# The substitution of every chunk on GpSimd, two transposes of each as ScalarE copies, and the weights converted by their bits

## The chip, the core and the metric

One core of a Trainium2 chip runs the whole program. Its engines work side by side, each through its own queue in order: TensorE (PE; its weight loads are counted apart as PEld), VectorE (DVE), ScalarE (ACT) and GpSimd (POOL); SyncE (SP) issues the transfers. The metric is the time of one execution on the device in microseconds; lower is better.

## The reference

Two parts. The first is a linear attention with a decaying state of 40 x 40 for each of 4 x 8 heads, over 768 time steps:

```python
for t in range(S):
    y[:, :, t] = np.einsum('bhd,bhde->bhe', rt, state)
    Sa = np.einsum('bhde,bhe->bhd', state, at)
    state_decay = state * wt[:, :, None, :] - np.einsum('bhd,bhe->bhde', Sa, bt)
    state = state_decay + np.einsum('bhd,bhe->bhde', vt, kt)
```

The second takes y, laid out as x of (4, 768, 320), through a gated block: h = gelu(x @ w_in) of width 1024, split in halves u and v; v is normalized over its 512 columns and mixed over the 768 time steps by w_sg, with a bias; the result is x + (u * v) @ w_out. The weights w_in and w_out come as doubles (as pairs of 32-bit words) and are used as a high and a low part of 32 bits.

## The kernel before

**Chunks.** Time is cut into NCH = 12 chunks of C = 64 steps. In a chunk the 64 dependent steps become small matrix products and one triangular inverse for each of the 32 heads; two heads lie on the 128 partitions, so that 16 pairs lie side by side. The state goes from chunk to chunk.

**Gates.** For each chunk c and batch entry b (four a chunk) a gate is made, from `gate_w` to `gate_k`: a scan for the running products of the decays (`ex`), a reciprocal, products `at` and `kb` (each a VectorE or a GpSimd instruction, by a letter V or G in a table), then products on TensorE into `ab`, two masks back into `at` on VectorE (`gate_a`), the negated triangle `nts` on ScalarE (`gate_n`) and `kbt` (`gate_k`). `gate_3` ends with the load of the inputs of the gate four places later (`load_main`), which SyncE issues when that buffer is free.

**The inverse.** `inv_in` transposes `nts` into `n` on VectorE (all 16 pairs at once) and sets `x` to ones on the diagonal. Forward substitution of 32 steps then runs on `x`: `steps(c, lo, hi, eng, cuts, nm)` gives the steps lo to hi - 1 for one engine. On VectorE, the first steps (below ROWS[0] = 12) and the last (from 26) are single instructions that multiply and add (x<-n,x and x<-x,n in the profile); between them, and on GpSimd always, a step is a product into `tv` or `tg` and a sum. `both` puts the first FIRST = 3 steps of a chunk on VectorE, the next up to 29 on GpSimd, and the last LAST = 2 go to VectorE from `plan`. `inv_back` turns the result: k = 0 transposes `x` into `x1z`, k = 1 transposes that into the upper columns of `xt`, k = 2 and k = 3 transpose 32 partitions each into its lower columns. `inv_g` and `inv_x` make the remaining quarter of the 64 x 64 inverse by products (`gp`, `xp`).

**The chain of states.** `chain1` to `chain5` make, for each b, the corrected values (`ru`, `vu`), the new state (`sp`, `sc`) and the outputs (`pq`, `pqs`, `yp`, `yt`), which go to memory as `xd`.

**Order.** Each engine's order is written out by hand: every piece has a position in a table (CH, GPOS, START, BACK, GX), 28 units to a chunk, and `half` sorts them. The pieces before the first chunk's main part stand in one `merge`: `early` places the gates of chunks 0 and 1, `both` chunk 1's substitution, `zeros` and `blanks` the fills of buffers, at positions such as T0, T2, SECOND. Gates run about two chunks ahead of the chain, the inverse about one.

**The second part.** While the last three chunks run, `Mlp.side` loads and converts the twelve pieces of w_in (`DEC` gives each a position and the engine of its tail, `DSTEP` the positions of its stages), and starts on v. The rest (`run`) goes through a written sequence of products (`hv`, `hu`, `sg`, `op`), with eight pieces of w_out converted between (`OUTS`, `OSTEP`, `OUTE`). `split64` converts one piece: its words in `stg`, an exponent field cut out and clamped into `sc`, the upper fraction bits made a number by ScalarE and multiplied by the scale, the high part `h` taken by a rounding copy on ScalarE, and the rest added up as the low part `l`.

The profile calls nearly all instructions line 117, the helper `call` that keeps each engine in program order, so that tiles tell them apart.

Of the kernel before, what the change touches and what calls it, by code (L numbers as in the profile page):

```python
# [1072 lines left out]
```

## Time and profile before

| | |
|---|---|
| median of 3 runs | 689.81 us (689.4 to 694.77) |
| the profiled execution | 690.71 us |
| its span in the profile | 688.9 us |
| mean granted clock of TensorE | 0.906 |
| PE busy | 581.5 us (84%) |
| DVE busy | 561.5 us (82%) |
| ACT busy | 375.7 us (55%) |
| POOL busy | 363.0 us (53%) |

The shares are means over stages that differ: the start (0 to about 85 us), the steady chunks (to about 340), the last chunks beside the first pieces of the second part (to about 400), and the second part. Windows, timelines and waits are therefore read stage by stage. Times in the timelines are us from the span's start; a bracket behind a row gives the idle time of its engine before it, and what ended that.

### The profile page before, as it was taken

To read this page: it belongs to the slowest core of one execution; us is meant where nothing else is said; L and a number is where in the kernel's file an instruction comes from. 1 tells how busy PE (TensorE), PEld (TensorE's weight loads), DVE (VectorE), ACT (ScalarE), POOL (GpSimd) and SP (SyncE) were. 2 spreads that over 40 slices of the span, in tenths; PEclk is the share of its full clock that TensorE was granted. 3 is DMA by queue.
4 is the path that set the end of the run, shared out by engine and by line. 5 is a ranking of instruction groups with operands and counts; after the bars stand their busy time and mean duration, and the time that the engine had idled before them with its cause. 6 is when DMAs were issued, how large, how long until landed. Compare 5 with 4: busy or idle time off the path is not lost.

```text
span 688.9 us, 22501 instructions
## 1 busy us (share of the span) xinstructions
PE 581.5 (84%) x8950; PEld 523.2 (76%) x8950; DVE 561.5 (82%) x1294; ACT 375.7 (55%) x1082; POOL 363.0 (53%) x767
## 2 busy tenths in 40 slices
PE   6336798989989898898959788786699999999996
PEld 5235677877878777787848677685599999999995
DVE  7999889989889898898979776888868668766842
ACT  5445766968768687686654633652335324524410
POOL 5217687676866868567682552554632333233321
PEclk8556599999999999999978898978699999999998
DMA  6632233334433344332334332250003000200001
GB/s 219 208 96 64 66 93 109 108 89 112 126 102 108 89 120 115 99 90 70 97 99 117 100 88 69 81 152 9 19 18 99 1 30 20 78 30 2 29 24 40
DMA packets 57618, 56.55 MB, mean 82 GB/s; under 512 B 35936, under 2 KB 47456, under 8 KB 57504
## 3 DMA queue, kind: packets, MB, share of 16 engines
q1 hardware_dynamic: 57504, 55.02, 27.9%
q8 instruction: 72, 1.18, 0.7%
q14 instruction: 42, 0.34, 0.2%
HBM read 47.14 MB, written 7.86 MB: 80 GB/s over the span
## 4 chain that ended last, share of the span: by engine, by line
PE 41%; DVE 35%; ACT 11%; issue 5%; DMA 4%; POOL 2%; SPq 1%; POOLq 0%; DVEq 0%; ACTq 0%
PE sg L117 12%; PE op L117 6%; PE hu L117 5%; PE hv L117 5%; DVE at L117 4%; DVE x L117 4%; DVE sc L117 4%; PE ab L117 4%; PE yp L117 3%; DVE ex L117 3%; ACT nts L117 3%; DVE fixed L117 2%; DVE n L117 2%; PE sp L117 2%; DVE xt L117 2%
## 5 line engine op out<-in xcount | busy, mean ns | idle before, releaser
L117 POOL TENSOR_TENSOR tg<-x,n 128x126 f32<-128x126 f32 (+19 forms) x288 | 109.8, 381 | 76.8 <-DVE x L117 55.1
L117 POOL TENSOR_TENSOR x<-x,tg 128x126 f32<-128x126 f32 (+19 forms) x288 | 114.1, 396 | 22.6
L117 POOL TENSOR_TENSOR gx<-g,gy 128x384 fp32r<-128x384 f32 x32 | 33.4, 1047 | 79.5 <-ACT gy L117 79.5
L117 ACT ACTIVATE nts<-ab 32x256 f32<-32x256 f32 x192 | 62.0, 323 | 23.0 <-DVE at L117 20.7
L117 PE MATMUL ab<-at,kb 64*64 64x64 f32 x1536 | 42.5, 246 | 35.8 <-POOL kb L117 14.2
L117 PE MATMUL sg<-wsh,vh 128*128 128x384 f32 x192 | 67.0, 349 | 4.5 <-ACT vh L117 4.5
L117 PEld LDWEIGHTS ab<-at,kb 64*64 64x64 f32 x1536 | 34.6, 153 | 44.6 <-POOL kb L117 15.9
L117 PE MATMUL sg<-wsh,vl 128*128 128x384 f32 x192 | 67.0, 349 | 1.7 <-POOL vl L117 1.7
L117 PE MATMUL sg<-wsl,vh 128*128 128x384 f32 x192 | 66.9, 348 | 0.6 <-POOL wsl L117 0.6
L117 PE MATMUL pq<-rt,vut 128*128 128x128 f32 x384 | 58.8, 299 | 7.3 <-ACT kbt L117 4.1
L117 PEld LDWEIGHTS pq<-rt,vut 128*128 128x128 f32 x384 | 49.9, 202 | 12.6 <-ACT kbt L117 6.2
L117 PE MATMUL yp<-pqs,kbt 128*64 128x64 f32 x768 | 49.7, 234 | 6.7 <-DVE pqs L117 3.8
L117 ACT COPY vs<-sc 64x160 f32<-64x160 f32 x88 | 28.3, 321 | 46.2 <-DVE sc L117 45.1
L117 ACT CAST gy<-g 128x384 fp32r<-128x384 f32 x32 | 16.4, 513 | 66.8 <-DVE g L117 66.8
L117 PEld LDWEIGHTS yp<-pqs,kbt 128*64 128x64 f32 x768 | 42.1, 146 | 9.7 <-PE ut L117 3.8
L117 PE MATMUL yp<-rt,s 80*40 80x64 f32 x704 | 46.2, 231 | 0.0
L117 ACT CAST vh<-v 128x512 fp32r<-128x512 f32 x24 | 14.9, 621 | 56.2 <-DVE v L117 56.2
L117 DVE SCALAR_TENSOR_TENSOR g<-sg,gl,bt 128x384 f32<-128x384 f32 x32 | 19.7, 615 | 29.4 <-PE sg L117 28.4
L117 POOL TENSOR_TENSOR vl<-v,vh 128x512 fp32r<-128x512 f32 x24 | 31.3, 1304 | 21.9 <-ACT vh L117 21.9
L117 PEld LDWEIGHTS sg<-wsh,vh 128*128 128x128 f32 x192 | 37.9, 197 | 5.4 <-ACT vh L117 5.2
L117 POOL TENSOR_TENSOR rs<-rs,mhalf 128x1 f32<-128x1 f32 x24 | 13.4, 560 | 53.7 <-DVE rs L117 49.1
L117 PE MATMUL ru<-rhsb,xt 64*64 64x40 f32 x768 | 31.1, 239 | 12.4 <-ACT xt L117 11.2
(142 smaller groups left out, 1719.8 us busy)
## 6 DMA issues: line engine op xcount, KB each, us to landing
main<-main SPq DMA_DIRECT2D x88, 160.8 KB
vu<-vs SPq DMA_DIRECT2D x24, 160.0 KB
vs<-vb SPq DMA_DIRECT2D x24, 160.0 KB
rt<-rt SPq DMA_DIRECT2D x48, 80.0 KB
vut<-vt SPq DMA_DIRECT2D x24, 160.0 KB
xd<-yt SPq DMA_DIRECT2D x96, 40.0 KB
xt<-xd SPq DMA_DIRECT2D x16, 192.0 KB
out<-y SPq DMA_DIRECT2D x16, 192.0 KB
```

The costliest lines, as they stand in the source:

```text
L117: return self.tc.keep_in_program_order(f(*a, **k))
```

## The change

Three things, and the tables that place them.

1. **Substitution.** FIRST becomes 0 and T1, CUT0 and FIRST1 go: GpSimd does steps 0 to 28 of every chunk, chunk 0 and 1 too, VectorE the last two of each. In the part before the main loop VectorE makes chunk 1's gates with all their products, and the gates of b = 0 and 1 of chunk 2 (which leave the main loop's first rows of GPOS). The fills of `blanks` are placed from position 0 on.
2. **Transposes.** `inv_back` for k = 2 and 3 copies 32 partitions of `xt` from its upper to its lower columns on ScalarE, in place of the transposes from `x1z` on VectorE; k = 3 moves from position 18.09 to 24.7.
3. **Weights.** `split64` takes the magnitude of the upper word on ScalarE, clamps and shifts it, and puts sign and fraction together so that the word itself is a number; the multiplication of the upper part and the conversion of its fraction are gone. The stages are six in place of seven.

```diff
-FIRST = 3
-FIRST1 = 1
+FIRST = 0
-T1 = 16.9
-TB0 = 4.75
-TB1 = 12.31
-CUT0 = (0, 5, 16)
+TB0 = 0.0
+TB1 = 4.5
-BACK = (17.18, 23.28, 26.9, 18.09)
+BACK = (17.18, 23.28, 26.9, 24.7)
-DSTEP = ((-9.0, 0.0, 0.7, 1.4, 1.6, 2.4, 2.8), (-9.0, 0.0, 0.7, 1.4, 2.4, 4.0, 4.6))
+DSTEP = ((-9.0, -1.0, 0.0, 0.7, 1.4, 2.4), (-9.0, -1.0, 0.0, 0.7, 1.4, 3.0))
...
-                V.transpose(out=xt[r, :, 0:32], in_=x1_of[c][r])
+                A.copy(out=xt[r, :, 0:32], in_=xt[r, :, 32:64])
...
         merge(early(0, 0, EX[0], E0A, E0K, 1.0),
-              [(T0, lambda: inv_in(0))],
-              spread(steps(0, 0, 31, V, CUT0, "tv"), T0 + 0.05, T1),
-              early(1, T2, EX[1], E1A, E1K, EW),
-              both(1, FIRST1, *SECOND, "tw"),
+              both(0, 0, T0, 0.01),
+              early(1, T2, EX[1], "VVVV", "VVVV", EW),
+              both(1, 0, SECOND, 0.01),
+              early(2, THIRD, EX[1], "VV", "VV", EW),
               spread(zeros(), ZERO, ZERO + 1), spread(bl, TB0, TB1))
...
+        for f in steps(0, 31 - LAST, 31, V, (0, 16), "tv"):
+            f()
...
-                jobs = [(c + 3, 1)] if hf else [(c + 2, b) for b in ((0, 1, 2, 3) if c == 0 else (2, 3))] + [(c + 3, 0)]
+                jobs = [(c + 3, 1)] if hf else [(c + 2, b) for b in (2, 3)] + [(c + 3, 0)]
...
+        def size():
+            sc = z["sc"] = self.tmp("sc", n, I32)
+            A.activation(out=sc.bitcast(F32), in_=z["x"].bitcast(F32)[:, 1:2 * n:2], func=AF.Abs)
+
         def fields():
-            V.tensor_scalar(out=sc, in0=hi, scalar1=20, scalar2=0x7FF,
-                            op0=ALU.logical_shift_right, op1=ALU.bitwise_and)
-            V.tensor_scalar(out=sc, in0=sc, scalar1=896.0, scalar2=1151.0, op0=ALU.max, op1=ALU.min)
+            V.tensor_scalar(out=sc.bitcast(F32), in0=sc.bitcast(F32), scalar1=HI_MIN, scalar2=HI_MAX,
+                            op0=ALU.max, op1=ALU.min)
+            V.tensor_scalar(out=sc, in0=sc, scalar1=3, scalar2=0x3FFFFFF8,
+                            op0=ALU.logical_shift_left, op1=ALU.bitwise_and)
...
-            V.tensor_scalar(out=sc, in0=sc, scalar1=896.0, scalar2=float(2 ** 23), op0=ALU.subtract, op1=ALU.mult)
-            V.scalar_tensor_tensor(out=sc, in0=hi, scalar=-2 ** 31, in1=sc, op0=ALU.bitwise_and, op1=ALU.bitwise_or)
-            V.tensor_scalar(out=hi, in0=hi, scalar1=0xFFFFF, scalar2=None, op0=ALU.bitwise_and)
+            V.scalar_tensor_tensor(out=hi, in0=hi, scalar=-2 ** 30, in1=sc, op0=ALU.bitwise_and, op1=ALU.bitwise_or)
+            V.tensor_scalar(out=sc, in0=hi, scalar1=-2 ** 23, scalar2=None, op0=ALU.bitwise_and)
...
-            A.activation(out=z["m"], in_=z["x"][:, 1:2 * n:2], func=AF.Copy, scale=2.0 ** -20, bias=1.0)
             A.activation(out=z["r"], in_=z["lt"], func=AF.Copy, scale=2.0 ** -36)
-        def scaled():
-            s = z["sc"].bitcast(F32)
-            G.tensor_tensor(out=z["m"], in0=z["m"], in1=s, op=ALU.mult)
-            G.tensor_tensor(out=z["r"], in0=z["r"], in1=s, op=ALU.mult)
-        def high():
             A.copy(out=h, in_=z["m"])
         def low():
+            G.tensor_tensor(out=z["r"], in0=z["r"], in1=z["sc"].bitcast(F32), op=ALU.mult)
             G.tensor_tensor(out=z["m"], in0=z["m"], in1=h.bitcast(F32), op=ALU.subtract)
             G.tensor_tensor(out=l, in0=z["m"], in1=z["r"], op=ALU.add)
```

(In `split64`, G is the engine that the tables name for the piece: GpSimd or VectorE. OSTEP loses an entry in the same way as DSTEP, SECOND becomes one position, 14.0, and THIRD = 14.1 is new; GPOS and GE lose the two gates of chunk 2.)

VectorE's order behind the n of chunk 0, at the start of the program (nts_94 is chunk 0's triangle; ex_138, at_154 and main_85 belong to the first gate of chunk 1). Before:

```order
L117 STREAM_TRANSPOSE n<-nts_94 128x32x32
L117 SCALAR_TENSOR_TENSOR x<-n,x 128x31
L117 TENSOR_SCALAR call<-ex_138 128x4
L117 RECIPROCAL fixed_83<-call 128x4
L117 SCALAR_TENSOR_TENSOR x<-n,x 128x30
L117 SCALAR_TENSOR_TENSOR x<-n,x 128x29 x2
```

After:

```order
L115 STREAM_TRANSPOSE n<-nts_94 128x32x32
L115 TENSOR_SCALAR call<-ex_138 128x4
L115 RECIPROCAL fixed_83<-call 128x4
L115 TENSOR_TENSOR at_154<-main_85,ex_138 128x4x64
L115 SCALAR_TENSOR_TENSOR fixed_84<-main_85,fixed_83 128x260
L115 TENSOR_TENSOR kb<-main_85,fixed_84 128x2x4x64
```

The steps of the substitution have left this place, and the gate's two products, at and kb, have come to it from GpSimd.

GpSimd's order at its first step of a substitution; kbt_112 is the last buffer of the blank fills. Before, the chain that begins here is chunk 1's, from its second step on:

```order
L117 MEMSET kbt_112 128x24
L117 TENSOR_TENSOR tg_718<-x,n 128x30
L117 TENSOR_TENSOR x<-x,tg_718 128x30
L117 TENSOR_TENSOR tg_721<-x,n 128x58
L117 TENSOR_TENSOR x<-x,tg_721 128x2x29
```

After, it is chunk 0's, from its first:

```order
L115 MEMSET kbt_112 128x24
L115 TENSOR_TENSOR tg_407<-x,n 128x31
L115 TENSOR_TENSOR x<-x,tg_407 128x31
L115 TENSOR_TENSOR tg_410<-x,n 128x30
L115 TENSOR_TENSOR x<-x,tg_410 128x30
```

One chain more stands in GpSimd's queue, and each is longer by the steps that VectorE had.

ScalarE's order in a steady chunk, between the copies of the state (vs) of one pair of batch entries and the triangle (nts) of the next gate. Before:

```order
L117 COPY vs_114<-sc_122 64x4x40 x2
L117 COPY vut_130<-ut 80x4x64
L117 COPY gs_119<-gp 32x512 x2
L117 COPY vs_114<-sc_123 64x4x40 x2
L117 COPY vut_130<-ut 80x4x64
L117 ACTIVATE nts_96<-ab_2549 32x256
```

After:

```order
L115 COPY vs_114<-sc_122 64x4x40 x2
L115 COPY vut_130<-ut 80x4x64
L115 COPY gs_119<-gp 32x512 x2
L115 COPY xt_90<-xt_90 32x16x32
L115 COPY vs_114<-sc_123 64x4x40 x2
L115 COPY vut_130<-ut 80x4x64
L115 COPY xt_90<-xt_90 32x16x32
L115 ACTIVATE nts_96<-ab_2511 32x256
```

The two copies in place of the transposes stand in this stretch of ScalarE's queue, one behind gs and one ahead of nts.

More of the change, by code (lines that the diff above doesn't have):

```diff
@@ L30 @@
 DECAY_LOW = 1e-09
-FIRST = 3
-FIRST1 = 1
+HI_MIN = float(np.uint32(896 << 20).view(np.float32))
+HI_MAX = float(np.uint32(1151 << 20).view(np.float32))
+FIRST = 0
 EW = 1.41
@@ L35 @@
 T0 = 6.16
-T1 = 16.9
 T2 = 5.9
-TB0 = 4.75
-TB1 = 12.31
-CUT0 = (0, 5, 16)
+TB0 = 0.0
+TB1 = 4.5
 CH = ((0.37, 2, 4, 5.28, 4.96, 7.81, 8.16, 12.17, 3.28, 10.76, 13.17, 14.9), (-0.13, 1.6, 7.06, 5.51, 8.13, 6.96,
     10.2, 10.99, 2.92, 8, 12, 13.85))
-GPOS = (((0.34, 0.33, 0.61, 1.31, 3.87, 4.25, 4.26, 4.27), (2.6, 2.59, 2.87, 3.57, 5.89, 6.51, 6.52, 6.53), (5.06,
+GPOS = (((5.06,
     5.05, 5.33, 6.03, 8.35, 10.4, 10.41, 10.42), (8.18, 8.17, 8.83, 9.53, 11.85, 12.47, 12.48, 12.49), (10.81, 10.8,
@@ L47 @@
     2.69, 9.57, 13.23, 13.24, 13.25),), ((1.07, 1.06, 1.26, 1.42, 9.29, 11.98, 11.99, 12.0),))
-GE = ("VVVVV", "VVV", "V", "V")
+GE = ("VVV", "VVV", "V", "V")
 START = (13.13, 0.58)
@@ L51 @@
 E0K = "GVGG"
-E1A = "GGGG"
-E1K = "GVGG"
-BACK = (17.18, 23.28, 26.9, 18.09)
+BACK = (17.18, 23.28, 26.9, 24.7)
 GX = (24.68, 4.6)
@@ L75 @@
 OUTS = (10, 11, 12, 13, 14, 15, 16, 17)
-OSTEP = (-2, 0, 0, 0, 0, 1, 1)
+OSTEP = (-2, 0, 0, 0, 0, 1)
 SGE = "GVGVGVGVVVGG"
 OUTE = "GGGVGGGG"
-SECOND = (18.63, 0.02)
+SECOND = 14.0
+THIRD = 14.1
 ZERO = 4.0
@@ L520, in early @@
             out = []
-            for b in range(B):
+            for b in range(len(EA)):
                 for f, x in zip(PIECES, X):
@@ L684, in load @@
             self.Q.dma_start(out=z["x"], in_=src)
+        def size():
+            sc = z["sc"] = self.tmp("sc", n, I32)
+            A.activation(out=sc.bitcast(F32), in_=z["x"].bitcast(F32)[:, 1:2 * n:2], func=AF.Abs)
         def fields():
-            x = z["x"]
-            hi = x[:, 1:2 * n:2]
-            sc = z["sc"] = self.tmp("sc", n, I32)
-            V.tensor_scalar(out=sc, in0=hi, scalar1=20, scalar2=0x7FF,
-                            op0=ALU.logical_shift_right, op1=ALU.bitwise_and)
-            V.tensor_scalar(out=sc, in0=sc, scalar1=896.0, scalar2=1151.0, op0=ALU.max, op1=ALU.min)
+            sc = z["sc"]
+            V.tensor_scalar(out=sc.bitcast(F32), in0=sc.bitcast(F32), scalar1=HI_MIN, scalar2=HI_MAX,
+                            op0=ALU.max, op1=ALU.min)
+            V.tensor_scalar(out=sc, in0=sc, scalar1=3, scalar2=0x3FFFFFF8,
+                            op0=ALU.logical_shift_left, op1=ALU.bitwise_and)
         def scale():
@@ L699, in scale @@
                             op0=ALU.logical_shift_right, op1=ALU.bitwise_and)
-            V.tensor_scalar(out=sc, in0=sc, scalar1=896.0, scalar2=float(2 ** 23), op0=ALU.subtract, op1=ALU.mult)
-            V.scalar_tensor_tensor(out=sc, in0=hi, scalar=-2 ** 31, in1=sc, op0=ALU.bitwise_and, op1=ALU.bitwise_or)
-            V.tensor_scalar(out=hi, in0=hi, scalar1=0xFFFFF, scalar2=None, op0=ALU.bitwise_and)
+            V.scalar_tensor_tensor(out=hi, in0=hi, scalar=-2 ** 30, in1=sc, op0=ALU.bitwise_and, op1=ALU.bitwise_or)
+            V.tensor_scalar(out=sc, in0=hi, scalar1=-2 ** 23, scalar2=None, op0=ALU.bitwise_and)
         def parts():
             z["m"], z["r"] = z["x"].bitcast(F32)[:, 1:2 * n:2], z["lt"].bitcast(F32)
-            A.activation(out=z["m"], in_=z["x"][:, 1:2 * n:2], func=AF.Copy, scale=2.0 ** -20, bias=1.0)
             A.activation(out=z["r"], in_=z["lt"], func=AF.Copy, scale=2.0 ** -36)
-        def scaled():
-            s = z["sc"].bitcast(F32)
-            G.tensor_tensor(out=z["m"], in0=z["m"], in1=s, op=ALU.mult)
-            G.tensor_tensor(out=z["r"], in0=z["r"], in1=s, op=ALU.mult)
-        def high():
             A.copy(out=h, in_=z["m"])
         def low():
+            G.tensor_tensor(out=z["r"], in0=z["r"], in1=z["sc"].bitcast(F32), op=ALU.mult)
             G.tensor_tensor(out=z["m"], in0=z["m"], in1=h.bitcast(F32), op=ALU.subtract)
             G.tensor_tensor(out=l, in0=z["m"], in1=z["r"], op=ALU.add)
-        return load, fields, scale, parts, scaled, high, low
+        return load, size, fields, scale, parts, low
     def weights_in(self):
```

## The prediction, made before the result was known

> **What bounds the kernel now.** I read the windows of each stage first (columns: stretch, length, then busy time of PE, PEld, DVE, ACT, POOL, granted clock, DMA share, GB/s).
>
> ```profile
> 55.30:86.60 31.30, 25.68 (x460) 22.17 (x460) 28.33 (x63) 21.64 (x69) 22.32 (x60) 0.61 0.25 76
> 201.80:230.30 28.50, 25.70 (x656) 22.36 (x653) 26.45 (x61) 21.48 (x69) 20.18 (x53) 1.00 0.39 106
> 340.40:376.00 35.60, 27.55 (x602) 24.75 (x598) 29.96 (x77) 16.16 (x46) 22.47 (x51) 0.81 0.39 107
> 460.00:496.00 36.00, 24.43 (x106) 20.44 (x105) 31.68 (x69) 14.09 (x40) 21.08 (x33) 0.83 0.06 15
> 496.00:540.00 44.00, 44.00 (x231) 42.51 (x230) 34.19 (x68) 19.36 (x40) 13.55 (x15) 0.94 0.16 50
> ```
>
> VectorE (DVE) is the fullest engine up to 496 us; from there TensorE is busy in all 44.00 of 44 us, and its work is not changed. So what is won before 496 us moves the end one for one, and nothing after it does. One period of the scan (a chunk) is 28.5 us.
>
> Next the timeline of VectorE at the start (start, length, instruction, idle before it):
>
> ```profile
> 19.74 2.13 DVE L117 STREAM_TRANSPOSE n<-nts 128x1024 f32<-128x1024 f32 x1 [0.29 <-ACT nts L117]
> 49.09 2.53 DVE L117 SCALAR_TENSOR_TENSOR x<-x,n 128x14 f32<-128x14 f32 x15
> 54.23 1.04 DVE L117 STREAM_TRANSPOSE x1z<-x 128x512 f32<-128x512 f32 x1
> 57.34 0.69 DVE L117 TENSOR_TENSOR_SCAN ex<-main,fixed 128x260 f32<-128x260 f32 x1
> 60.02 0.69 DVE L117 TENSOR_TENSOR_SCAN ex<-main,fixed 128x260 f32<-128x260 f32 x1
> 62.91 0.74 DVE L117 TENSOR_TENSOR at<-ab,mask 64x256 f32<-64x256 f32 x2
> 85.51 1.07 DVE L117 STREAM_TRANSPOSE x1z<-x 128x512 f32<-128x512 f32 x1
> ```
>
> From the end of n (21.9) to the fifteen last small steps (49.09 + 2.53 = 51.6 us) VectorE does chunk 0's whole substitution and, between its steps, the gates of chunk 1. The row x1z marks the end of a chunk's substitution: chunk 0 at 54.23, chunk 1 at 85.51. GpSimd (POOL) meanwhile:
>
> ```profile
> 54.39 0.23 POOL L117 TENSOR_TENSOR tg<-x,n 128x30 f32<-128x30 f32 x1 [14.15 <-DVE x L117]
> 55.02 0.28 POOL L117 TENSOR_TENSOR tg<-x,n 128x58 f32<-128x58 f32 x1
> 79.62 0.28 POOL L117 TENSOR_TENSOR x<-x,tg 128x45 f32<-128x45 f32 x1
> 84.33 0.28 POOL L117 TENSOR_TENSOR tg<-x,n 128x56 f32<-128x56 f32 x1 [4.43 <-DVE x L117]
> 138.98 0.28 POOL L117 TENSOR_TENSOR tg<-x,n 128x56 f32<-128x56 f32 x1 [4.34 <-DVE x L117]
> ```
>
> It stands idle for 14.15 us before 54.39, and some 4.3 us in each period, waiting for VectorE's first steps.
>
> **The start.** Chunk 1's 28 steps took GpSimd 54.39 to 79.90 = 25.5 us (0.455 us an instruction, gaps included). One more step like the first, 0.63 us (54.39 to 55.02), makes a full chain of 29 steps 26.1 us. After the change it starts for chunk 0 when n is there, at 22.0 (the blank fills that are moved earlier stand in its idle time before that), and ends at 48.1. VectorE now makes chunk 1's four gates and two of chunk 2's meanwhile. A gate costs 57.34 to 60.02 = 2.7, and 0.7 for its two masks: 3.4 us. Six gates and one n (2.1) from 21.9 make 44.4; for the waits on ACT before n and on TensorE before the last masks I add 3.6, an estimate: 48. The two engines arrive together, and x1z of chunk 0 comes at 49.3 in place of 54.23. SyncE's queue now has the loads of two more gates (which wait for those gates' kb) ahead of chunk 0's vs, rt and vut; these leave at 46 to 52 us, as the first products ask for them, and I price that at 0 to 2 us.
>
> GpSimd goes on with chunk 1: 48.1 + 26.1 = 74.2, three last VectorE steps (0.9), x1z at 75.1 in place of 85.51. VectorE is there sooner: of the 31.3 us between its two x1z, two gates (6.8), two transposes (1.35) and four small steps (0.75; their rows follow) are gone, 49.3 + 22.4 = 71.7. So GpSimd ends last, and the start is worth **-10.4 us** (bounds -12, if the waits that follow chunk 1 shrink too, and -4, if TensorE, at a clock of 0.61 here and 25.68 of 31.30 us busy, paces it).
>
> **The steady periods.** What leaves VectorE in each:
>
> ```profile
> 201.85 0.70 DVE L117 STREAM_TRANSPOSE xt<-x1z 32x512 f32<-32x512 f32 x1
> 206.40 0.42 DVE L117 TENSOR_TENSOR yt<-yp,ex 128x256 f32<-128x256 f32 x1 [1.32 <-PE yp L117]
> 206.74 0.69 DVE L117 STREAM_TRANSPOSE xt<-x1z 32x512 f32<-32x512 f32 x1
> 223.13 0.23 DVE L117 SCALAR_TENSOR_TENSOR x<-n,x 128x31 f32<-128x31 f32 x1
> 223.62 0.68 DVE L117 SCALAR_TENSOR_TENSOR x<-n,x 128x30 f32<-128x30 f32 x3
> ```
>
> Transposes 1.35, steps 0.75 (their ends overlap what follows): 2.1 us of 28.5, with one idle gap of 1.32. What comes to ACT has no row; the nearest are its copies of as many elements:
>
> ```profile
> L117 ACT COPY xt<-xp 32x512 f32<-32x512 f32 x24 | 13.8, 573 | 2.3 <-PE xp L117 2.0
> L117 ACT COPY x<-x 128x512 f32<-128x512 f32 x12 | 7.4, 621 | 0.2
> ```
>
> 0.57 to 0.62 each; I take 0.58 with the first, 1.15 us a chunk. How much of the 2.1 shows is read from who waits:
>
> ```profile
> 196.17 1.32 ACT L117 ACTIVATE nts<-ab 32x256 f32<-32x256 f32 x4 [1.42 <-DVE at L117]
> 209.97 0.40 ACT L117 COPY at<-at 64x256 f32<-64x256 f32 x1 [0.30 <-DVE at L117]
> 211.42 0.78 PE L117 MATMUL ab<-at,kb 64*64 64x64 f32 x32 [0.69 <-ACT rhsb L117]
> 224.66 0.38 ACT L117 ACTIVATE nts<-ab 32x256 f32<-32x256 f32 x1 [1.23 <-DVE at L117]
> 203.54 0.67 PE L117 MATMUL sp<-vu,kbt 128*64 128x40 f32 x16
> 204.39 0.32 DVE L117 TENSOR_TENSOR sp<-sp,sc 104x160 f32<-104x160 f32 x1
> ```
>
> The four steps stand just ahead of the masks for which ACT waits 1.42: their 0.75 moves ACT, and TensorE behind it, forward in full. The first transpose lies beside a stretch where TensorE runs through to its sp, which ends at 204.2, 0.2 us before VectorE takes it up: only that much of the 0.70 is won. Then the two ACT copies come between the copies after gp and the nts that follow; ACT runs there without a gap up to 209.97, where its slack is 0.30. So TensorE's ab at 211.42, which waits for ACT, does not come forward by 0.9 but stays within 0.1, and VectorE, early by 1.5, waits there for about 1.0. At the end of the period all are ahead by 0.25 + 0.75 = **1.0 us**. From x1z of chunk 1 to that of chunk 10 there are nine periods: **-9.0 us** (bounds 0 and 9 x 2.1 = -19). GpSimd's chain of 26.1 fits the 27.5 that are left.
>
> ```profile
> 339.32 1.09 DVE L117 STREAM_TRANSPOSE x1z<-x 128x512 f32<-128x512 f32 x1
> ```
>
> **Conversion, and the last chunks.** Each of 20 pieces loses one VectorE instruction, and one multiplication on the engine that does its tail:
>
> ```profile
> L117 DVE TENSOR_SCALAR sc<-sc 128x256 int32<-128x256 int32 x32 | 13.7, 429 | 0.6
> L117 DVE TENSOR_TENSOR stg<-stg,sc 128x256 f32<-128x256 f32 x6 | 2.8, 468 | 3.6 <-ACT stg L117 3.6
> L117 POOL TENSOR_TENSOR stg<-stg,sc 128x256 f32<-128x256 f32 x10 | 8.6, 863 | 29.1 <-ACT stg L117 21.6 <-DMA xd<-yt 7.4
> ```
>
> That is at most 16 x 0.43 + 6 x 0.47 = 9.7 us of VectorE. ACT keeps its three instructions a piece (the magnitude replaces a conversion of the same size: nothing), but the high half is ready without the trip to the multiplying engine and back. Where it counts:
>
> ```profile
> 346.75 0.43 DVE L117 TENSOR_TENSOR stg<-stg,sc 128x256 f32<-128x256 f32 x1 [1.60 <-ACT stg L117]
> 349.93 0.43 DVE L117 TENSOR_TENSOR stg<-stg,wih 128x256 f32<-128x256 f32 x1 [1.57 <-ACT wih L117]
> 356.90 0.43 PE L117 MATMUL ru<-rhsb,xt 64*64 64x40 f32 x2 [6.75 <-ACT xt L117]
> 388.22 0.39 PE L117 MATMUL ru<-rhsb,xt 64*64 64x40 f32 x2 [4.06 <-ACT xt L117]
> ```
>
> TensorE stands 6.75 us because ACT's xt is queued behind the conversion of the second weight, which waits for VectorE. VectorE gets there earlier by two transposes (1.4), two small instructions (0.7), one multiplication (0.4) and one of the two ACT waits (1.6): 4.1, of which I count all, and 2 of the 4.06: **-6 us** (bounds 0 and -10.8, both stalls). Chunk 11's chain then ends near where VectorE asks for it, so more is not likely. Between 460 and 496 us VectorE is busy 31.68 of 36, with most of the w_out pieces there; their removed instructions are 3 to 4 us, of which I take **-3** (bounds 0 and -5).
>
> **Sum.** The profiled execution took 690.71 us (span 688.9). 690.7 - 10.4 - 9.0 - 6 - 3 = 662.3. That execution lies 0.9 above the median of the runs, 689.81, so I say **662**.
>
> **Rivals.** *GpSimd in VectorE's way.* Some VectorE instructions are longer beside a GpSimd one:
>
> ```profile
> 209.33 0.61 DVE L117 TENSOR_TENSOR at<-main,ex 128x256 f32<-128x256 f32 x1
> 225.89 0.41 DVE L117 TENSOR_TENSOR at<-main,ex 128x256 f32<-128x256 f32 x1
> ```
>
> The at at 225.89 came soon after a pause of GpSimd, the one at 209.33 in the middle of its chain; the pause shrinks from 4.3 to about 1 us. If five VectorE instructions a chunk lose 0.2 each, the period gains 1.0 - 1.0 = 0: 690.7 - 10.4 - 0 - 9 = 671, and with a start slowed alike 675. Against it: GpSimd is running beside most of them already. The Trainium skill, "SBUF — State Buffer", section "Who interferes with whom", says that a VectorE instruction with two SBUF inputs and a GpSimd one that reads SBUF exclude each other for a whole instruction; the two rows agree with it, and by it the time would be this rival's 671.
>
> *VectorE alone sets the time.* If the ACT copies hide, the whole 2.1 shows: 690.7 - 12 - 19 - 6 - 5 = 649. For it: 26.45 of 28.5 busy; against it: ACT's slack of 0.30.
>
> *GpSimd becomes the bound: slower.* If half of the 58 instructions of a chain met a VectorE one and lost 0.2, a chain took 31.9, the period 3.4 more, ten times: +34, the start +1, less 9 later: 717. From 12 such meetings a chunk (2.4 / 0.2) on GpSimd paces the period; from about 25 on the whole gain is lost. Against it: the chain of 54.39 to 79.90 ran beside a VectorE busy 28.33 of 31.30 us, and its 0.455 us is in my sum. The Trainium skill, "GPSIMD Engine Reference", section 3.1, has GpSimd about twice as slow as VectorE at such work; the chain's own rows set my price, and the rule only says that the work is not cheaper there.
>
> *The start does not gain* (TensorE at half clock or the loads pace it): 690.7 - 4 - 9 - 9 = 669.
>
> **How the numbers follow.** Chances: forecast 0.48 (655 to 668), GpSimd in VectorE's way 0.20 (668 to 677), start 0.10 (667 to 673), VectorE alone 0.15 (643 to 655), GpSimd the bound 0.05 (about 717), some mixture that cancels 0.02. A measurement of this kernel tells about 1% from no change. Faster by over 1% (below 683) is 0.92, within 1% 0.04, slower 0.04. The range that leaves out no more than 2 in 10 is 648 to 676.
>
> **What would show it.** Right: a first tg at 22 us and no pause before the second chain; x1z of chunk 0 near 49, of chunk 1 near 75, of chunk 10 near 320; a period near 27.5 with a new wait of VectorE for ab about ten us after x1z, and ACT without a gap before it; the stall before ru at the last chunk down to some 2 us; full TensorE from about 468 us. Wrong: a period of 28.5 or more, at of 0.61 throughout, an instruction of tg well above 0.46, or a start in which x1z of chunk 1 waits for anything but GpSimd.

## The result

The changed kernel takes 671.66 us in the median of its first four runs (668.41 to 674.49), the kernel before 691.14 in the runs beside them: a ratio of 0.971, 95% interval 0.964 to 0.978. Four later runs of it on another occasion gave 669.64 us, 0.971 again (0.965 to 0.977). The forecast was 662 in a range of 648 to 676.

The profile below is that of the run of 674.49 us (span 672.7), the longest of the eight; a second profile, of a run of 666.78 (span 665.0), stands beside it where the two differ. First the windows by stage (the columns are those of the prediction).

```profile
20.00:50.00 30.00, 13.87 (x216) 10.93 (x216) 25.00 (x53) 17.07 (x57) 22.68 (x61) 0.50 0.51 155
50.00:83.00 33.00, 27.37 (x454) 23.99 (x455) 21.86 (x44) 18.73 (x58) 27.08 (x75) 0.50 0.27 80
83.00:111.00 28.00, 26.62 (x560) 23.35 (x562) 21.82 (x50) 22.45 (x70) 19.28 (x53) 0.84 0.31 86
111.00:330.00 219.00, 202.93 (x5187) 177.87 (x5189) 192.52 (x425) 179.07 (x559) 172.78 (x464) 1.00 0.39 105
330.00:400.00 70.00, 62.12 (x1046) 56.04 (x1040) 44.04 (x115) 38.57 (x107) 34.98 (x68) 0.71 0.39 108
```

The same view of the second profile, three of its stages:

```profile
50.00:83.00 33.00, 27.53 (x455) 24.16 (x456) 21.70 (x44) 18.58 (x57) 27.09 (x75) 0.50 0.28 81
83.00:111.00 28.00, 25.67 (x619) 21.99 (x619) 24.15 (x54) 22.72 (x71) 20.99 (x58) 0.99 0.38 103
330.00:400.00 70.00, 59.54 (x1013) 53.24 (x1010) 47.87 (x121) 41.05 (x112) 34.44 (x67) 0.78 0.37 101
```

VectorE is no longer the fullest engine: from 50 to 83 us it is busy 21.86 of 33, and TensorE at half clock 27.37. The steady part does the same in both profiles; they differ where the granted clock does, from 83 to 111 and from 330 to 400 us.

Where the time went is read from marks that every profile has: the start of x1z of some chunks (VectorE's timeline), the first hv (TensorE's) and the span's end, in us.

| kernel | x1z chunk 0 | 1 | 2 | 10 | 11 | first hv | end |
|---|---|---|---|---|---|---|---|
| before | 54.23 | 85.51 | 115.23 | 339.32 | 372.56 | 408.61 | 688.9 |
| after, first profile | 49.82 | 79.68 | 111.41 | 327.77 | 358.23 | 394.32 | 672.7 |
| after, second profile | 49.66 | 79.52 | 109.11 | 325.34 | 355.98 | 388.38 | 665.0 |

From these come the terms of the prediction's sum. It took 10.4 up to chunk 1, and nine periods from there; here the first of these nine stands with the start.

| term | forecast | first profile | second profile |
|---|---|---|---|
| start, to x1z of chunk 2 | -11.4 | -3.8 | -6.1 |
| eight periods, chunk 2 to 10 | -8.0 | -7.7 | -7.9 |
| last chunks, chunk 10 to hv | -6 | -2.7 | -6.3 |
| w_out part, hv to the end | -3 | -1.9 | -3.7 |
| sum, from the marks unrounded | -28.4 | -16.2 | -23.9 |

The start is short in both. The other three are close to the forecast in the second profile. The forecast's -28.4 set beside the -19.5 of the first medians (691.14 to 671.66) and the -22.0 of the later ones (691.65 to 669.64) leaves 6 to 9 us to explain.

In the start GpSimd does what was said. Its chains, from its timeline:

```profile
22.55 0.50 POOL L115 TENSOR_TENSOR tg<-x,n 128x31 f32<-128x31 f32 x1 [5.79 <-DVE call L115]
49.05 0.24 POOL L115 TENSOR_TENSOR tg<-x,n 128x31 f32<-128x31 f32 x1
75.22 0.24 POOL L115 TENSOR_TENSOR tg<-x,n 128x31 f32<-128x31 f32 x1 [0.18 <-DVE n L115]
```

Chunk 0's chain starts at 22.55, chunk 1's follows at 49.05 without a pause, chunk 2's at 75.22: 26.2 us for chunk 1's, 26.1 forecast. But VectorE takes the end of chunk 1's up only at 78.91:

```profile
49.82 1.05 DVE L115 STREAM_TRANSPOSE x1z<-x 128x512 f32<-128x512 f32 x1
53.86 0.69 DVE L115 TENSOR_TENSOR kb<-main,fixed 128x512 f32<-128x512 f32 x1
62.42 0.33 DVE L115 TENSOR_TENSOR sp<-sp,sc 104x160 f32<-104x160 f32 x1 [7.87 <-PE sp L115]
78.91 0.73 DVE L115 SCALAR_TENSOR_TENSOR x<-x,n 128x15 f32<-128x15 f32 x3
79.68 1.07 DVE L115 STREAM_TRANSPOSE x1z<-x 128x512 f32<-128x512 f32 x1
84.86 0.33 DVE L115 TENSOR_TENSOR sp<-sp,sc 104x160 f32<-104x160 f32 x1 [1.89 <-PE sp L115]
88.23 0.33 DVE L115 TENSOR_TENSOR sp<-sp,sc 104x160 f32<-104x160 f32 x1 [2.67 <-PE sp L115]
111.41 1.09 DVE L115 STREAM_TRANSPOSE x1z<-x 128x512 f32<-128x512 f32 x1
```

It stands 7.87 us for sp of chunk 0, the end of a serial chain x1z, gp, xp, ru, sp that goes back and forth between TensorE and ACT. TensorE's timeline shows the chain:

```profile
51.08 1.93 PE L115 MATMUL ru<-vs,at 64*64 64x40 f32 x32 [2.41 <-DMA vs<-vb]
52.94 1.92 PE L115 MATMUL gp<-x1z,nts 64*32 64x32 f32 x64
55.53 0.31 PE L115 MATMUL xp<-xt,gs 64*32 64x32 f32 x2 [0.67 <-ACT gs L115]
58.76 0.43 PE L115 MATMUL ru<-rhsb,xt 64*64 64x40 f32 x2 [0.72 <-ACT xt L115]
61.22 1.08 PE L115 MATMUL sp<-vu,kbt 128*64 128x40 f32 x16
```

Two things in it could be shorter: gp stands behind the ru that waited for the load of vs until 51.08 (x1z was there at 50.87), and each product runs at a clock of 0.50.

### The profile page after: what moved, and what is told of

Same layout as the page of the kernel before. It is cut to its first block, busy times and chain, and to the rows that moved or that the text cites. A ratio compares the mean times of both kernels' runs of the same rounds, so it can differ in the third digit from the quotient of the medians.

```text
span 672.7 us, 22391 instructions
## 1 busy us (share of the span) xinstructions
PE 593.0 (88%) x8950; PEld 535.2 (80%) x8950; DVE 510.7 (76%) x1100; ACT 391.5 (58%) x1106; POOL 383.3 (57%) x866
## 5 line engine op out<-in xcount | busy, mean ns | idle before, releaser
L115 POOL TENSOR_TENSOR tg<-x,n 128x126 f32<-128x126 f32 (+21 forms) x348 | 127.8, 367 | 47.7 <-DVE n L115 10.6
L115 POOL TENSOR_TENSOR x<-x,tg 128x126 f32<-128x126 f32 (+21 forms) x348 | 133.6, 384 | 27.3
L115 PE MATMUL ab<-at,kb 64*64 64x64 f32 x1536 | 45.2, 250 | 30.3 <-DVE kb L115 17.0
L115 PEld LDWEIGHTS ab<-at,kb 64*64 64x64 f32 x1536 | 36.1, 156 | 40.7 <-ACT junk L115 14.0
L115 PE MATMUL pq<-rt,vut 128*128 128x128 f32 x384 | 61.6, 310 | 0.8 <-DVE yt L115 0.6
L115 PEld LDWEIGHTS pq<-rt,vut 128*128 128x128 f32 x384 | 53.2, 214 | 4.0 <-DVE yt L115 1.2
L115 ACT COPY vs<-sc 64x160 f32<-64x160 f32 x88 | 28.3, 321 | 38.6 <-DVE sc L115 37.7
L115 POOL TENSOR_TENSOR vl<-v,vh 128x512 fp32r<-128x512 f32 x24 | 31.3, 1303 | 21.5 <-ACT vh L115 21.3
L115 DVE TENSOR_TENSOR at<-ab,mask 64x256 f32<-64x256 f32 x96 | 35.9, 407 | 7.8 <-PE ab L115 7.3
```

Of the source, the lines that this page charges most:

```text
L115: return self.tc.keep_in_program_order(f(*a, **k))
```

## The experiments

Ratios are to the kernel before, run beside each on the same chip, with 95% intervals. "The changed kernel" has 0.971.

### The start

**The two gates of chunk 2 back behind chunk 0's x1z.**

```diff
-              early(2, THIRD, EX[1], "VV", "VV", EW),
...
-                jobs = [(c + 3, 1)] if hf else [(c + 2, b) for b in (2, 3)] + [(c + 3, 0)]
+                jobs = [(c + 3, 1)] if hf else [(c + 2, b) for b in ((0, 1, 2, 3) if c == 0 else (2, 3))] + [(c + 3, 0)]
```

(with their rows of GPOS and GE)

> The two early gates of chunk 2 go back behind x1z of chunk 0, everything else as after the change. Theory (behind x1z of chunk 0 the serial chain x1z, gp, gs, xp, xt, ru, vu, sp of 12.6 us sets the time, and VectorE stands 7.9 us in it): the two gates fill that idle time, x1z of chunk 0 comes at 46 to 50 us, x1z of chunk 1 within 1.5 us of the 79.7 measured, x1z of chunk 2 within 2 us of 111.4, and the whole within 2 us of the changed kernel. Rival (the gates moved ahead are a true gain of the start, and what is late is late for another cause): x1z of chunk 1 near 86 and the whole 6 to 7 us slower than the changed kernel, about 0.980 of the kernel before.

667.83 us, 0.967 (0.962 to 0.972), which can't be told from 0.971. x1z of chunk 1 comes at 79.68, to the hundredth as in the first profile of the changed kernel, that of chunk 2 at 109.25, near the second's 109.11. VectorE now makes the gates where it stood, and its wait for sp is 0.60 us in place of 7.87. So the 6.8 us of gates that the prediction took off VectorE there brought nothing: behind chunk 0's x1z not VectorE's work but the chain to sp sets the time, and the gates had only covered it. One thing more moves with them: without the two gates' loads ahead of it the load of vs is issued at 34.53 us in place of 46.85 (SyncE's timeline), and the first ru is out of gp's way. What that is worth is seen two runs below.

**Eight fillers a gate.** `warmup(8)`, eight products of a tile of zeros, behind each gate of chunks 0 and 1.

```diff
+            if c < 3 and FILL[c]:
+                warmup(FILL[c])
```

> Eight filler matmuls behind each gate of chunks 0 and 1, whose result nobody uses, to keep TensorE busy and its granted clock up. Theory (the half clock between 21 and 103 us lengthens the serial chain and paces what follows): the granted clock between 50 and 83 us rises from 0.50 to 0.8 or more, the way from x1z to sp of chunk 0 falls from 12.6 to 9 or 10 us, x1z of chunk 2 comes 4 to 6 us earlier than 111.4, and the whole is 4 to 8 us faster than the changed kernel. Rival (the clock is not what paces the start, or is not moved by fillers): clock and chain stay as they are and the whole is the same or 1 to 3 us slower for the fillers in the way.

671.23 us, 0.970 (0.964 to 0.975): no gain that can be told. The granted clock is 0.80 from 20 to 50 us, but 0.51 from 50 to 83: it fell in TensorE's pause of 5.21 us ahead of 42.91, before the chain began. x1z to sp stays at 12.6 us. The experiment did not make the condition that it was to test, and says nothing on the theory.

**The first ru behind gp.**

```diff
-        for b in range(2):
-            chain1(0, b)
...
         inv_g(0)
+        for b in range(2):
+            chain1(0, b)
         inv_x(0)
```

> The first two products ru of chunk 0, which wait for the load vs until 51.08 us, go behind gp on TensorE (and their copies behind gs on ACT). Theory (gp stands 2.0 us behind them, 52.94 in place of 50.9, and the chain to sp is bare): sp of chunk 0 comes at 60.4 to 61 in place of 62.4, x1z of chunk 1 at 77.5 to 78.5, x1z of chunk 2 earlier by 0 to 2 us than the 108.5 of the earlier experiments, the whole 0 to 2 us faster than the changed kernel. Rival (the products only move the same time to another place, behind gp they hold up xp): sp within 0.5 us of 62.4 and the whole unchanged.

gp starts at 50.84, and VectorE's rows are:

```profile
60.85 0.33 DVE L115 TENSOR_TENSOR sp<-sp,sc 104x160 f32<-104x160 f32 x1 [6.48 <-PE sp L115]
68.04 0.33 DVE L115 TENSOR_TENSOR sp<-sp,sc 104x160 f32<-104x160 f32 x1 [1.23 <-PE sp L115]
```

sp is 1.6 us earlier, x1z of chunk 1 comes at 77.93, of chunk 2 at 107.27, as the theory had it. With the gates still early and the ru out of the way x1z of chunk 1 is 1.75 us ahead of the 79.68 that the run with late gates has too. By these marks the early gates bring that much at most, and in the changed kernel the late vs takes it back. The whole, 668.44 us or 0.972 (0.967 to 0.978), can't tell 1.6 us: its four runs reach from 664.22 to 672.09.

**Fillers up to gp.** With the ru moved, fillers now also in the pauses of 5.2 and 2.6 us.

```diff
+FILL = {(0, 0): 8, (0, 1): 8, (0, 2): 8, (0, 3): 8, (1, 0): 8, (1, 1): 8, (1, 2): 8, (1, 3): 24, (2, 1): 10}
...
+            if (c, b) in FILL:
+                warmup(FILL[c, b])
```

> As the run before, and TensorE is kept busy with fillers from the first gate until gp of chunk 0, the pauses of 5.2 and 2.6 us too in which the clock fell in the run with eight fillers. Theory (the half clock from 42 to 83 us is what makes the chain of chunk 0 and the waits of VectorE until x1z of chunk 2 long): granted clock above 0.9 from 25 to 60 us, the way from x1z to sp of chunk 0 below 9 us, x1z of chunk 1 at 74 to 76, x1z of chunk 2 at 104 to 106, the whole 3 to 5 us faster than the run before. Rival (VectorE's own order paces it): clock full, the chain shorter, but x1z of chunk 2 within 1 us of the run before, and the whole too.

664.06 us, 0.965 (0.962 to 0.969), 4.4 us below the run before it; the intervals still overlap. VectorE's timeline:

```profile
59.49 0.33 DVE L116 TENSOR_TENSOR sp<-sp,sc 104x160 f32<-104x160 f32 x1 [5.43 <-PE sp L116]
76.76 1.10 DVE L116 STREAM_TRANSPOSE x1z<-x 128x512 f32<-128x512 f32 x1
104.26 1.08 DVE L116 STREAM_TRANSPOSE x1z<-x 128x512 f32<-128x512 f32 x1
```

The clock is 1.00 from 30 to 40 and from 50 to 55 us and 0.58 from 55 to 60: it held for the first half of the chain, which takes 10.2 us, not below 9 as expected, and x1z of chunk 1 comes at 76.76, not at 74 to 76. But x1z of chunk 2 comes at 104.26, 11.0 us before that of the kernel before, nearly the start of the forecast (-11.4). This is one profile: the same start stands in a later run, and there x1z of chunk 2 comes at 109.71 (below).

### The steady periods

**One copy, no copy.** The line below for k = 3 alone (one copy left), and for k = 2 and 3 (no copy).

```diff
-BACK = (17.18, 23.28, 26.9, 24.7)
+BACK = (17.18, 23.28, 26.9, 18.09)
...
-                A.copy(out=xt[r, :, 0:32], in_=xt[r, :, 32:64])
+                V.transpose(out=xt[r, :, 0:32], in_=x1_of[c][r])
```

> Of the two ACT copies, k = 3 goes back to a VectorE transpose at position 18.09; k = 2 stays on ACT. Theory (in the steady period ACT's queue is the path through nts and ab, so a copy there gives back most of what the transpose saved): the period stays within 0.3 us of 27.45 us, and comes out at 27.1 to 27.5; the whole 0 to 4 us faster than the changed kernel. Rival (VectorE's own work sets the period): 0.7 us more a period, 28.1, and the whole 6 us slower.

> Both transposes back on VectorE, ACT copies neither; the substitution stays on GpSimd in full. Theory: the two copies are worth 0.25 us a period, the steps 0.75, so the period is 27.6 to 27.8 us and the whole about 2 us slower than the changed kernel. Rival (VectorE's own work sets the period): 1.35 us more a period, 28.8, and the whole about 12 us slower.

**The steps back on VectorE.** `FIRST = 3` from chunk 2 on, both copies kept.

> From chunk 2 on the first three steps of a substitution are VectorE's again, the two copies stay on ACT. As the prediction had it, these steps are worth 0.75 us a period: 28.2 in place of 27.45, and the whole 7 us slower than the changed kernel. Rival (VectorE has idle time of 2 us or more behind x1z in each period, so what it does in addition is partly hidden): a period of 27.7 to 28.0 and 2 to 5 us slower. Second rival (GpSimd, off VectorE's way for longer, gives it all back): a period of 27.5 and no change.

The period (from one x1z to the next, chunks 2 to 9, seven of them): the most frequent value, the odd ones, and the mean.

| | first steps on VectorE | all steps on GpSimd |
|---|---|---|
| both transposes on VectorE | 28.5, two 28.9; mean 28.62 (before) | 28.2, two 27.4; mean 27.99 |
| one copy on ACT | not run | 27.9, one 28.3; mean 27.94 |
| both copies on ACT | 28.2, two 28.5; mean 28.30 | 27.45, two 27.8; mean 27.55 (after) |

The whole: one copy 670.74 us, 0.971 (0.966 to 0.976); no copy 669.47, 0.968 (0.963 to 0.973); steps back 675.90, 0.981 (0.975 to 0.986), 6.3 us above the changed kernel in the same comparison. Only the last can be told from the changed kernel: its four runs (674.02 and up) are all slower than the four beside it (673.86 at most), though the intervals touch. Of the first two the period says what the time cannot.

For one copy the theory missed (27.1 to 27.5 expected, 27.94 measured), and the rival's 28.1 was nearer; for no copy both missed, the theory by 0.2 (27.6 to 27.8 expected, 27.99 measured) and the rival, with 28.8, by more. For the steps the price of the prediction held: 28.30 less 27.55 is 0.75.

The mean is what adds up to the time. By it the steps are worth 0.63 us alone and 0.75 beside the copies, the copies 0.32 alone and 0.44 beside the steps, and both together 1.07, against a forecast of 0.75, 0.25 and 1.0. Only some 0.1 us of a period comes from having both. The most frequent values alone would say that either edit is worth 0.3 first and 0.75 second, because they leave out the odd periods.

Why most periods with the steps alone gain only 0.3 is seen in the kernel without copies, which has periods of 28.24 and of 27.40 us with the same instructions. The groups of VectorE in a period of 28.24 (192.69 to 220.93), and then in one of 27.40 (249.15 to 276.55):

```profile
L115 DVE TENSOR_TENSOR at<-main,ex 128x256 f32<-128x256 f32 x4 | 2.3, 582 | 0.0
L115 DVE TENSOR_SCALAR call<-ex 128x4 f32<-128x4 f32 x4 | 1.4, 347 | 0.1
```

```profile
L115 DVE TENSOR_TENSOR at<-main,ex 128x256 f32<-128x256 f32 x4 | 2.0, 491 | 0.0
L115 DVE TENSOR_SCALAR call<-ex 128x4 f32<-128x4 f32 x4 | 0.9, 213 | 0.1
```

(at and call are two instructions of a gate.) Four at of 582 ns in place of 491 and four call of 347 in place of 213 make 4 x 0.091 + 4 x 0.134 = 0.90, about the whole difference of 0.84; idle time is the same 1.3 us (for yp) in both. Which engine begins first decides. The third call of a short period (108.83 to 136.24) and the third of a long one (192.69 to 220.93), each with GpSimd's instruction beside it:

```profile
124.73 0.17 DVE L115 TENSOR_SCALAR call<-ex 128x4 f32<-128x4 f32 x1
124.76 0.37 POOL L115 TENSOR_TENSOR tg<-x,n 128x96 f32<-128x96 f32 x1
```

```profile
209.03 0.39 POOL L115 TENSOR_TENSOR x<-x,tg 128x96 f32<-128x96 f32 x1
209.07 0.37 DVE L115 TENSOR_SCALAR call<-ex 128x4 f32<-128x4 f32 x1
```

GpSimd is busy beside both. In the first VectorE begins 0.03 us ahead and has its 0.17 us; in the second it begins 0.04 us behind GpSimd, and ends 0.02 us behind it. This holds throughout: in all 14 profiles every call between 111 and 330 us with a row of its own that took 0.20 us or more ended 0.01 to 0.04 us behind the GpSimd instruction within which it began. The kernel without copies has 26 such calls of 30, the changed kernel 18. In its two short periods two of the four calls have 0.17, in its five long ones none. So the rival "GpSimd in VectorE's way" is real: in five of seven periods it takes 0.84 us of what the steps gave. What puts the two engines in one order or the other was not tried.

### The weights

**The old conversion.** `split64`, DSTEP and OSTEP as in the kernel before, all else as after it.

> The conversion of the weights and its stages as before the change, the substitution and the two copies as after it. Theory (the conversion is worth the last chunks' 2.5 to 3 us and the 2 to 3 of the w_out part): x1z of chunk 10 as in the changed kernel, x1z of chunk 11 and the first hv 2 to 4 us later, the whole 4 to 6 us slower than the changed kernel, about 0.977 of the kernel before. Rivals: 9 us or more slower (the conversion carries all the gain of the last part), or no change (its gain comes from the transposes alone).

674.12 us, 0.978 (0.974 to 0.982): 0.007 of 691, some 5 us, above the changed kernel, as expected (by the two intervals anything from 0 to 10). x1z of chunk 10 comes at 325.68, near the second profile's 325.34; from there to hv it takes 67.4 us (second profile 63.0, first 66.6, before 69.3), from hv to the end 279.1 (276.6, 278.4 and 280.3). To hv, kernels with the same last chunks lie between 62.1 and 66.6 in six profiles (the changed kernel's two, and those of the four runs on the start above), so this mark alone shows little. Clear of the scatter is the way from x1z of chunk 10 to that of chunk 11: 32.19 us, where these six have 30.46 to 30.70 and the kernel before 33.24. TensorE's wait for xt in it, and in the first profile of the changed kernel:

```profile
342.14 0.43 PE L115 MATMUL ru<-rhsb,xt 64*64 64x40 f32 x2 [6.52 <-ACT xt L115]
```

```profile
341.11 0.31 PE L115 MATMUL ru<-rhsb,xt 64*64 64x40 f32 x2 [3.65 <-ACT xt L115]
373.77 0.43 PE L115 MATMUL ru<-rhsb,xt 64*64 64x40 f32 x2 [3.76 <-ACT xt L115]
```

Of the 9 us that the prediction gave to this part the conversion carries some 5 by the whole time, and some 1.6 of the 2.6 us between the two x1z by the marks. That the rest comes with what is gone from VectorE beside it is argued, not shown.

**The magnitude on VectorE.** In the changed kernel VectorE's clamp waits for ACT's Abs (three of six such rows between 337 and 377 us, 11.8 us together):

```profile
337.83 0.82 DVE L115 TENSOR_SCALAR sc<-sc 128x256 f32<-128x256 f32 x2 [1.95 <-ACT sc L115]
370.97 1.08 DVE L115 TENSOR_SCALAR sc<-sc 128x256 f32<-128x256 f32 x2 [3.60 <-ACT sc L115]
376.58 0.62 DVE L115 TENSOR_SCALAR sc<-sc 128x256 f32<-128x256 f32 x2 [3.06 <-ACT sc L115]
```

```diff
-            A.activation(out=sc.bitcast(F32), in_=z["x"].bitcast(F32)[:, 1:2 * n:2], func=AF.Abs)
+            V.tensor_scalar(out=sc, in0=z["x"][:, 1:2 * n:2], scalar1=0x7FFFFFFF, scalar2=None, op0=ALU.bitwise_and)
```

(and its place in DSTEP 0.0 in place of -1.0)

> The magnitude of a piece's upper word is made on VectorE, by an and with 0x7FFFFFFF, in place of ACT's Abs. Theory (the new waits of VectorE for ACT's magnitude, 11.8 us in six pieces between 337 and 377 us, lie on the path): from x1z of chunk 10 to the first hv 64 us in place of 66.5, and the whole 2 to 4 us faster than the changed kernel. Rival (they lie beside TensorE's own work, or VectorE's extra instruction of 0.4 us for each of 20 pieces costs as much): the whole the same or 1 to 3 us slower.

665.63 us, 0.968 (0.964 to 0.972). These waits are gone, and the first stall of ru is 2.31 us; the second is 4.24, no shorter than before. From x1z of chunk 10 to that of chunk 11 it takes 28.55 us in place of 30.46 to 30.70 in the six profiles named above; to hv 60.2, below the 62.1 to 66.6 of all six. By its own time this can't be told from 0.971; in the next runs it can.

### Repeated, and both gains together

> The changed kernel itself once more, beside the runs below, so that they have it on the same chip. All theories: 0.968 to 0.974 of the kernel before. Of the 111.41 us at which x1z of chunk 2 came in its first profile the theory of the clock says that it was a late one, since seven other kernels with the same work up to there had 107 to 109: with full clock from about 83 us on it is 108 to 109.5, with half clock until 93 us again about 111.

669.64 us, 0.971. x1z of chunk 2 at 109.11, the clock full again from 83 us on, in place of 92: the 111.41 of the first profile goes with a late rise of the clock. Between chunk 10 and hv the two profiles of one and the same kernel differ by 3.5 us. The first profile, and then the second, from 380 to 390 us:

```profile
380.00:390.00 10.00, 10.00 (x137) 9.60 (x134) 5.73 (x16) 3.42 (x12) 3.83 (x6) 0.50 0.29 77
```

```profile
380.00:390.00 10.00, 9.74 (x173) 8.45 (x170) 6.35 (x18) 5.85 (x18) 5.77 (x8) 0.98 0.26 64
```

TensorE is full, or nearly so, in both, and gets through 137 products at one clock and 173 at the other.

**Fillers up to gp, the late ru, and the magnitude on VectorE:**

> The fillers and the late ru of an earlier run, and the magnitude of the weights on VectorE. Theory (the two gains, 4 to 7 us at the start and 2 to 4 us in the last chunks, stand at different places and add up): 0.958 to 0.964 of the kernel before, x1z of chunk 2 at 104 to 105, x1z of chunk 10 to that of chunk 11 28.5 us. Rival (the clock that TensorE loses at another place takes one of them back): 0.965 or more.

661.67 us, 0.957 (0.954 to 0.960), better than expected. Against the same without the magnitude, 0.965 (0.962 to 0.969), the intervals part: the magnitude's move is a gain. They part as well against the magnitude alone, 0.968 (0.964 to 0.972): fillers and late ru together are one too. (Both comparisons set ratios from two chips side by side.) Of the marks only one came as expected, x1z of chunk 10 to that of chunk 11 with 28.47 us. x1z of chunk 2 comes at 109.71, not at 104 to 105, although the start is that of the run with 104.26. The last fillers ran at half clock and held gp up until 52.84 (x1z was there at 50.96), and the clock was full only from 90 us on. So its profile doesn't show the gain of the start, and whether its other runs have it is not known.

**Thirteen fillers more:**

```diff
+FILLB = {(3, 0): 5}
...
         inv_x(0)
+        warmup(3)
```

(and `(2, 2): 5` in FILL)

> As the run before, with 13 more fillers between 53 and 72 us, three of them behind xp, five behind the products of chunk 2's third gate and five ahead of those of chunk 3's first. Theory (the clock falls at 54 us because TensorE's narrow products leave it too little work): granted clock above 0.9 until 75 us, the way from x1z to sp of chunk 0 shorter by 1 to 2 us, x1z of chunk 2 at 102 to 104, the whole 1 to 2 us faster than the run before. Rival (from here VectorE's order paces the start, or the fillers stand in the way): x1z of chunk 2 at 104 or later and no gain.

657.83 us, 0.952 (0.949 to 0.956), the fastest of all: 3.8 us below the run before it and some 12 below the changed kernel. The windows show the clock held until 70 us, and lost with the 2.27 us in which TensorE waited ahead of 73.97:

```profile
55.00:60.00 5.00, 4.38 (x106) 3.69 (x104) 0.35 (x2) 3.14 (x9) 4.17 (x11) 1.00 0.24 70
65.00:70.00 5.00, 4.24 (x89) 3.62 (x85) 4.46 (x8) 4.62 (x16) 4.22 (x11) 1.00 0.37 109
70.00:75.00 5.00, 2.73 (x43) 2.41 (x41) 4.90 (x12) 3.47 (x12) 3.98 (x14) 0.88 0.10 35
75.00:80.00 5.00, 5.00 (x62) 4.33 (x60) 2.87 (x5) 0.59 (x2) 3.98 (x14) 0.50 0.34 100
```

x1z to sp takes 9.5 us (11.2 in the run before), and x1z of chunk 1 comes at 75.56, right behind GpSimd's chain, as the prediction had it (75.1). x1z of chunk 2 comes at 107.18, later than the 102 to 104 expected: from 74 to 87 us the clock is at half again, and VectorE waits 1.89 and 2.67 us for sp, the same two numbers as in the first profile of the changed kernel.

This stretch goes with the clock's return in all profiles. Seven of them, whose edits to the start all lie ahead of the stretch (in us; windows of the granted clock):

| profile | clock full from | that is behind x1z of chunk 1 | x1z of chunk 1 to 2 |
|---|---|---|---|
| fillers up to gp | 76.3 | -0.4 | 27.5 |
| magnitude on VectorE | 80.9 | 1.9 | 28.7 |
| first ru behind gp | 80.5 | 2.6 | 29.3 |
| changed kernel, second | 83.5 | 4.0 | 29.6 |
| thirteen fillers more | 87.5 | 11.9 | 31.6 |
| fillers, ru and magnitude | 90.2 | 12.2 | 31.7 |
| changed kernel, first | 92.2 | 12.5 | 31.7 |

The longer the clock stays at half behind x1z of chunk 1, the longer the stretch, by 4 us in all. None of the edits tried steers the return: the earliest and one of the latest belong to the same start.

## Why the prediction was right and where it failed

*The start: too large, and the step that failed.* Forecast -10.4 by x1z of chunk 1 (-11.4 by that of chunk 2), measured -5.8 (85.51 to 79.68) and -3.8 or -6.1. Right were GpSimd's start at 22, its 26.1 us a chain, the absence of a pause and x1z of chunk 0 (49.8 for 49.3). The step that failed is "VectorE is there sooner": two gates, transposes and steps were taken off the 31.3 us between the two x1z, as if these were VectorE's work alone. They held a chain of TensorE and ACT of 12.6 us that the gates had covered. With the gates gone VectorE stood there 7.87 us, and took 29.9 us (49.82 to 79.68) in place of the 22.4. The late load of vs, which the prediction priced at 0 to 2 us, was 1.6 of it. The rest is the chain itself and TensorE's half clock, which no single number prices: with the ru late and fillers in the start x1z of chunk 2 came at 104.26 in one profile (-11.0), at 109.71 in another with the same start (-5.5), and at 107.18 with more fillers (-8.1), as the clock came back early or late. So the low bound (-4, "if TensorE paces it") was near the case, and of the rivals "the start does not gain" (669, chance 0.10), with the causes that it named, came nearest to the measured 670 to 672. It was given too little: the clock of 0.61 stood in the profile of before, and the later place of the load in the prediction's own text. The 671 of "GpSimd in VectorE's way" is as near only by chance, since by it the steady part would have gained nothing.

*The steady part: right, though the waits stand elsewhere.* -7.7 and -7.9 over eight periods, forecast -8.0. The path that was named, ACT without a gap, shows where it was expected:

```profile
198.85 0.62 ACT L115 COPY xt<-xt 32x512 f32<-32x512 f32 x1
200.55 0.62 ACT L115 COPY xt<-xt 32x512 f32<-32x512 f32 x1
201.19 1.32 ACT L115 ACTIVATE nts<-ab 32x256 f32<-32x256 f32 x4
```

VectorE's new waits stand elsewhere than forecast, behind x1z and not for ab (0.30 us at most, where about 1.0 was expected). In the period from 166.29 to 193.75 they are:

```profile
169.84 0.33 DVE L115 TENSOR_TENSOR sp<-sp,sc 104x160 f32<-104x160 f32 x1 [0.75 <-PE sp L115]
171.41 0.42 DVE L115 TENSOR_TENSOR yt<-yp,ex 128x256 f32<-128x256 f32 x1 [0.88 <-PE yp L115]
173.22 0.42 DVE L115 TENSOR_TENSOR yt<-yp,ex 128x256 f32<-128x256 f32 x1 [0.74 <-PE yp L115]
```

That is 2.37 us of idle time where the kernel before had 1.32 (the one wait for yp in the prediction's rows): 1.05 more, as much as the forecast had put ahead of ab. "Steps 0.75, transposes 0.25" comes out at 0.63 to 0.75 and 0.32 to 0.44 by the mean of the periods. What the sum left to a rival is VectorE's longer instructions beside GpSimd: in the changed kernel call took 0.229 us in the mean (0.218 before), without the copies 0.298, and there five of seven periods lost 0.84 us. No row of before told which of the two would come, so that they stayed away is luck.

*The last chunks and w_out: right in size in one profile.* -6.3 and -3.7 in the second profile for -6 and -3; -2.7 and -1.9 in the first, at a clock of 0.71 in place of 0.78 from 330 to 400 us. The stall of 6.75 us fell to 3.65, not to the forecast's 2: the new wait of VectorE for ACT's magnitude, which the prediction had at nothing ("the magnitude replaces a conversion of the same size"), stood there; moved to VectorE, 2.31. Of the second stall, 4.06, the forecast counted 2; it fell to 3.76.

*GpSimd as the bound* (717) did not come; chunk 1's chain took 26.2 us where this rival had 31.9. (Its limit of 12 meetings is that of the old period of 28.5; against the 27.5 of the forecast it would be 7.) *VectorE alone sets the time* (649) did not come either, but with fillers in the start and the magnitude moved a kernel with the same change takes 657.83.

*What stays open.* The eight runs of the changed kernel lie between 665.99 and 674.49 us, and the two profiles put their difference where the clock differs. Why TensorE's clock falls and returns at other times in runs of one kernel was not settled, so neither was how much of the forecast's 662 any single run can reach. Most kernels here have one profile, so a mark that hangs on the clock, of the start above all, can't be given to an edit by it alone.

## What to carry to other kernels

Work that is moved out of a stretch shortens it only if nothing serial lay under that work: before taking a duration off, look for the chain that ends last when it is gone, and price its hops at the clock of that stretch. To see whether two edits add, compare the mean of the periods, not the most frequent one: here they nearly add by the mean, and seem far from it by the other. Put the longer instructions beside a busy neighbour into the price of a move. Where TensorE idles in a phase of short dependent products, idle products in its pauses can be worth more than the scheduling around it: here 90 of them, with one product moved behind another, took the ratio from 0.968 to 0.957 on top of the magnitude's move, and 13 more brought another 3.8 us.

## What was not expected of the hardware

- **The clock needs more than a busy TensorE.** Windows of the first profile:

```profile
80.00:85.00 5.00, 5.00 (x63) 4.25 (x63) 2.19 (x4) 0.28 (x1) 4.14 (x12) 0.50 0.25 86
85.00:90.00 5.00, 5.00 (x112) 4.54 (x111) 1.98 (x7) 3.71 (x9) 4.22 (x11) 0.50 0.08 19
90.00:95.00 5.00, 5.00 (x140) 4.72 (x140) 4.47 (x10) 3.94 (x14) 4.22 (x11) 0.79 0.30 84
```

By the profile TensorE was busy without a pause from 72.6 to 92 us at a clock of 0.50, and only then was it full; in the second the same took from 72.4 to 83, with fillers and the late ru from 69.5 to 76, with these and the magnitude from 70.9 to 90, with more fillers from 74 to 87. The Trainium skill, "TensorE: Matmul & The Clock Gate", section "What's actually happening", gives one busy window of some 3.4 us for the rise; the profile of the kernel before comes near it (busy from 83.9, full from 87.9 us), these five took two to nearly six times as long, and the measurement decides.
- **It falls in different pauses.** With eight fillers a gate it fell in a pause of 5.2 us (ahead of 42.91), with the most fillers in one of 2.27 us (ahead of 73.97), but with the fillers up to gp also at about 55 us with no pause over 0.8 us, amid products of 64 x 32 and 64 x 40. With three fillers of 128 x 128 among these it held, but in another run without the three it fell only at 59 us, so that the three are not shown to be the cause. In the steady part (202.93 of 219 us busy) it never fell.
- **VectorE waits out the GpSimd instruction that it begins in.** The same 128 x 4 instruction of VectorE took 0.17 us where it began first and up to 0.47 where it began within one of GpSimd's, and the same period 27.40 or 28.24.
